# Both MLPs of a mixer from float16 parts, with the low-part matmuls one step behind

## The chip, the cores and the metric

The kernel runs on one core of a Trainium2 chip. The metric is device microseconds of one execution; the median of three executions stands for a kernel. The engines are named as in the profile: PE (TensorE, matmuls), PEld (its weight loads), DVE (VectorE), ACT (ScalarE), POOL (GpSimd) and SP (SyncE, which issues most DMAs). A program hands every engine its own list of instructions, which it works off in that order; semaphores make one engine wait for another.

## The reference

Four sequences of 768 positions and 384 features go through three layers. Only the two MLPs, which the change touches, are shown in full:

```python
# layer 1: linear attention with complex decay, y[t] = q[t] . S[t], S a 48x48 state per head
x = attention(q, k, v, a_re, a_im)            # (4, 768, 384)
# layer 2
u = x + (x^T @ U @ V)^T                        # U (768, 32), V (32, 768)
x = u + np.maximum(u @ w_ch1, 0.0) @ w_ch2     # w_ch1 (384, 1536), w_ch2 (1536, 384)
# layer 3, with its own w_ch1, w_ch2
u = x + real(fft(fft(x, axis=1), axis=2))
un = (u - mean(u)) / sqrt(var(u) + 1e-06)
out = u + np.maximum(un @ w_ch1, 0.0) @ w_ch2
```

The MLP weights, U and V come as float64, the rest as float32.

## The kernel before

**How an exact product is made.** An operand that needs more than one matmul pass of precision is split into a high part and the rest (hi + lo), both of type fp32r here, and a product is three matmuls: hi·hi, hi·lo, lo·hi. That is `mm3` (L91 to L95; the three matmuls are L93, L94, L95).

**The MLPs.** `moe_units` (L161) runs one MLP. The hidden width of 1536 is cut into 12 blocks `f` of 128, a sequence (`b`) into two halves `g` of 384 positions. For each (b, g, f), called a unit here: nine matmuls make the hidden block `hp` in PSUM (three blocks `k` of the input times `mm3`); ACT writes its positive part `hh` to SBUF (L191), DVE the remainder `hl` (L193); then `second` (L166) multiplies `hh` and `hl` with the block's second weight into three accumulators `acc` with nine more matmuls. `second` of a unit is issued after the nine `hp` matmuls of the next unit. A unit is 18 matmuls of 128 by 128 by 384; a pass (one b, one g) is 12 units, 216 matmuls; there are 16 passes, 3456 matmuls. `hp` has two PSUM banks, `hh` and `hl` two buffers each, `acc` three banks.

**What runs beside them.** The attention of the first sequence stands ahead of everything. During the first MLP's passes of sequence b the attention of sequence b+1 is worked in (`Side` counts out its steps, one or two a half unit), during the last sequence's passes the Fourier part `dft(0)`; during the second MLP's passes the Fourier part of the next sequence. `make_ut` and `make_un` build the input pairs `u` (hi, lo) of the next pass in its last units.

**The weights.** `load_w` (L138) brings half a block's weights: a DMA of float64 words `stw` (384 KB, into a ring of 5 buffers that the `u` pairs share), one ACT and three DVE operations that make a float32 `x` of them (L110, L132, L133; `x` is one of 3 buffers), an ACT copy that rounds the high part into `w` (L147) and a POOL subtraction for the low part (L148). There are 48 such loads, 24 for each MLP. A block's `w` tile (fp32r, high and low, both products) is one of 12 buffers, so all blocks of one MLP fill them: the second MLP's loads have to wait for the last pass of the first, where two a unit are asked for, and four come behind it.

**The order.** A list scheduler lays the instructions of each engine out in the order in which its own clock finds them ready, with `high_priority` for `hh` and `hl`. So work written later can come earlier on an engine that it finds free.

**At the end** `verdict` (L1012) counts range tests, each in a column of `stats`; only if one fails does a slow exact path (`recurrence`, `rest`) run.

## Time and profile before

| what | us |
|---|---|
| median of three executions (lowest, highest) | 1004.03 (1003.54, 1008.71) |
| the profiled execution, and its span in the trace | 1008.71, 1008.7 |
| attention of sequence 0, up to the first hp matmul | 0 to 139.6 |
| first MLP, sequences 0 to 2, with attention 1 to 3 | 139.6 to 553.4 |
| first MLP, sequence 3, and first pass of the second MLP | 553.4 to 708.3 |
| second MLP, its other seven passes, and the end | 708.3 to 1008.7 |
| PE, DVE, ACT, POOL busy over the span | 867.8, 643.1, 466.6, 224.9 |

The profiled execution is the slowest of the three, 4.7 us over the median. Busy time of PE counts matmuls that overlap as one stretch, so its share says where PE stood still, not how fast it went; that is read from the distance between starts of matmuls.

### The profile page before, as it was taken

To read this page: it belongs to the slowest core of one execution; us is meant where nothing else is said; L and a number is where in the kernel's file an instruction comes from. 1 tells how busy PE (TensorE), PEld (TensorE's weight loads), DVE (VectorE), ACT (ScalarE), POOL (GpSimd) and SP (SyncE) were. 2 spreads that over 40 slices of the span, in tenths; PEclk is the share of its full clock that TensorE was granted. 3 is DMA by queue.
4 is the path that set the end of the run, shared out by engine and by line. 5 is a ranking of instruction groups with operands and counts; after the bars stand their busy time and mean duration, and the time that the engine had idled before them with its cause. 6 is when DMAs were issued, how large, how long until landed. Compare 5 with 4: busy or idle time off the path is not lost.

```text
span 1008.7 us, 16225 instructions
## 1 busy us (share of the span) xinstructions
PE 867.8 (86%) x6350; PEld 821.9 (81%) x6350; DVE 643.1 (64%) x1110; ACT 466.6 (46%) x891; POOL 224.9 (22%) x227
## 2 busy tenths in 40 slices
PE   0056858798898898989999999799999999999997
PEld 0045747787887898878999999689999999999997
DVE  7967696767567796787873539986535635453121
ACT  8556557565775877768742223453112212211111
POOL 4312362302012010120205216532401312010000
PEclk9998677988998999989999999999999999999999
DMA  9049546463653627346055114341210101000000
GB/s 355 1 64 155 146 136 131 102 102 104 103 95 79 104 79 119 81 91 105 9 88 204 40 32 134 109 149 33 65 46 17 58 23 47 1 25 24 1 24 27
DMA packets 47093, 83.39 MB, mean 83 GB/s; under 512 B 5600, under 2 KB 36064, under 8 KB 47008
## 3 DMA queue, kind: packets, MB, share of 16 engines
q1 hardware_dynamic: 45152, 75.96, 33.3%
q0 software_dynamic: 1856, 6.31, 1.9%
q8 instruction: 52, 0.85, 0.4%
q14 instruction: 33, 0.27, 0.1%
HBM read 53.79 MB, written 9.44 MB: 63 GB/s over the span
## 4 chain that ended last, share of the span: by engine, by line
PE 46%; DVE 24%; DMA 13%; ACT 8%; issue 4%; SPq 4%; POOL 1%; another core or an unknown queue 0%; ACTq 0%; DVEq 0%; POOLq 0%
DMA QT<-QK 8%; PE acc L95 6%; PE hp L93 6%; PE hp L95 6%; PE hp L94 6%; PE acc L93 6%; PE acc L94 6%; DMA stw<-in_w_dram 5%; SPq L437 4%; PE sc L462 3%; DVE ls L354 2%; DVE QK L430 2%; DVE wxw L133 1%; ACT ls L89 1%; DVE wxw L132 1%
## 5 line engine op out<-in xcount | busy, mean ns | idle before, releaser
L193 DVE SCALAR_TENSOR_TENSOR hl<-hp,hh 128x384 fp32r<-128x384 f32 x192 | 105.6, 552 | 201.0 <-ACT hh L191 193.3
L191 ACT ACTIVATE hh<-hp 128x384 fp32r<-128x384 f32 x192 | 93.4, 488 | 273.9 <-PE hp L95 253.7
L93 PE MATMUL acc<-w,hh 128*128 128x384 f32 x576 | 204.0, 354 | 5.9 <-ACT hh L191 4.8
L94 PE MATMUL acc<-w,hh 128*128 128x384 f32 x576 | 198.8, 345 | 0.0
L95 PE MATMUL acc<-w,hl 128*128 128x384 f32 x576 | 164.7, 351 | 17.6 <-DVE hl L193 17.4
L95 PEld LDWEIGHTS acc<-w,hl 128*128 128x128 f32 x576 | 106.4, 194 | 23.6 <-DVE hl L193 23.1
L93 PEld LDWEIGHTS acc<-w,hh 128*128 128x128 f32 x576 | 111.8, 194 | 10.5 <-ACT hh L191 8.6
L94 PEld LDWEIGHTS acc<-w,hh 128*128 128x128 f32 x576 | 112.3, 195 | 0.2
L93 PE MATMUL hp<-u,w 128*128 128x384 f32 x288 | 101.2, 355 | 11.4 <-ACT u L639 11.4
L94 PE MATMUL hp<-u,w 128*128 128x384 f32 x288 | 103.2, 358 | 0.0
L95 PE MATMUL hp<-u,w 128*128 128x384 f32 x288 | 101.8, 353 | 0.0
L94 PE MATMUL hp<-n,w 128*128 128x384 f32 x288 | 96.5, 335 | 1.4 <-DVE n L917 1.2
L95 PE MATMUL hp<-n,w 128*128 128x384 f32 x288 | 96.5, 335 | 0.0
L93 PE MATMUL hp<-n,w 128*128 128x384 f32 x288 | 96.3, 335 | 0.0
L462 PE MATMUL sc<-QT 96*128 96x128 f32 x384 | 59.8, 311 | 28.7 <-DMA QT<-QK 23.5
L462 PEld LDWEIGHTS sc<-QT 96*128 96x128 f32 x384 | 55.1, 219 | 32.9 <-issue 30.3
L148 POOL TENSOR_TENSOR w<-wxw,w 128x384 fp32r<-128x384 f32 x48 | 57.5, 1202 | 75.1 <-ACT w L147 72.9
L93 PEld LDWEIGHTS hp<-u,w 128*128 128x128 f32 x288 | 57.7, 202 | 12.8 <-ACT u L639 12.8
L94 PEld LDWEIGHTS hp<-u,w 128*128 128x128 f32 x288 | 57.5, 200 | 1.1 <-DVE u L640 0.8
L95 PEld LDWEIGHTS hp<-u,w 128*128 128x128 f32 x288 | 57.3, 199 | 0.4
L94 PEld LDWEIGHTS hp<-n,w 128*128 128x128 f32 x288 | 54.1, 188 | 2.0 <-DVE n L917 2.0
L537 POOL TENSOR_SCALAR fe<-QT 96x8 f32<-96x8 f32 x20 | 6.5, 325 | 216.4 <-DMA QT<-QK 211.4
(285 smaller groups left out, 1747.3 us busy)
## 6 DMA issues: line engine op xcount, KB each, us to landing
QT<-QK SPq DMA_DIRECT2D x144, 129.0 KB
stw<-in_w_dram SPq DMA_DIRECT2D x48, 384.0 KB
ain<-in_a_dram SPq DMA_DIRECT2D x12, 768.0 KB
qkin<-in_qk_dram SPq DMA_DIRECT2D x12, 768.0 KB
x1d<-x SPq DMA_DIRECT2D x24, 192.0 KB
vin<-in_v_dram SPq DMA_DIRECT2D x18, 192.0 KB
lo<-x1d SPq DMA_DIRECT2D x12, 192.0 KB
out_dram<-lo SPq DMA_DIRECT2D x12, 192.0 KB
```

The lines of the kernel that those rows point to most:

```text
L89: ordered(lambda: A.activation(*args, **kw))
L93: T.matmul(o, ah, bh, start=start, stop=False, skip_group_check=skip)
L94: T.matmul(o, ah, bl, start=False, stop=False, skip_group_check=skip)
L95: T.matmul(o, al, bh, start=False, stop=stop, skip_group_check=skip)
L132: V.scalar_tensor_tensor(out=xi, in0=xi, scalar=3, in1=low, op0=ALU.logical_shift_left, op1=ALU.bitwise_or)
L148: G.tensor_tensor(w[:, 1, zs], x, f32(w[:, 0, zs]), ALU.subtract)
L191: A.activation(hh, hp, AF.Relu)
L193: V.scalar_tensor_tensor(out=hl, in0=hp, scalar=0.0, in1=f32(hh), op0=ALU.max, op1=ALU.subtract)
L354: V.tensor_tensor_scan(out=flat(s1), data0=starts, data1=flat(s1), initial=1.0, op0=ALU.max, op1=ALU.mult)
L430: V.tensor_tensor(QK[:, :, :, to], x[:, :, j].unsqueeze(1).to_broadcast([128, 2, 3, 128]), w, ALU.mult)
L437: nc.sync.dma_start(QT[p0 : p0 + 16], QK[:, z, i, :])
L462: T.matmul(ps[:, h, :], q[:, 128:256], q[:, :128], start=True, stop=True)
```

## The change

Both MLPs work on float16 parts instead of fp32r. Weights are scaled up before they are split (by 2^3 and 2^8, `WP`), the first MLP's input by 2^5 (`UP`), and the additions at the end scale back. For that each `load_w` has one more POOL operation, which scales `x` in place. The parts take half the room, so one buffer of `wpl` holds both MLPs' weights of a block (`wboth`), and the second MLP's loads are spread one a unit over sequence 3. New range tests: `check_v`, a square sum in `prelim`, and `check_w`, 48 DVE operations that square and sum the high parts. In `moe_units` the matmuls of `hl` go through a list `lows` and are issued one unit behind those of `hh`; `hl` has three buffers. The slow path keeps fp32r.

```diff
+    def hidden(name, tag):
+        if parts16[0]:
+            return moe.tile([128, 384], F16, tag=tag, name=name, bufs=3 if tag == "hl" else 2)
...
     def pair(name):
-        return moe.tile([128, 2, 384], F32R, tag="u", name=name, bufs=5)
+        return moe.tile([128, 2, 384], F16 if parts16[0] else F32R, tag="u", name=name, bufs=5)
...
     def load_w(mi, f, z, st=None):
-        if z == 0:
+        if z == 0 and not parts16[0]:
             wt[mi, f] = wpl.tile([128, 2, 768], F32R, tag="w", name=f"w{mi}_{f}")
+        elif z == 0:
+            if mi == 0:
+                wboth[f] = wpl.tile([128, 2, 2, 768], F16, tag="w", name=f"w{f}")
+            wt[mi, f] = wboth[f][:, mi]
...
-        A.copy(w[:, 0, zs], x)
-        G.tensor_tensor(w[:, 1, zs], x, f32(w[:, 0, zs]), ALU.subtract)
+        if parts16[0]:
+            A.activation(w[:, 0, zs], x, AF.Copy, scale=WP[z])
+            G.tensor_scalar(x, x, WP[z], 0.0, ALU.mult, ALU.add)
+            G.tensor_tensor(w[:, 1, zs], x, w[:, 0, zs], ALU.subtract)
...
+    def check_w(mi, f, z):
+
+        hi = wt[mi, f][:, 0, z * 384 : (z + 1) * 384]
+        unread = ft(f"chk{mi}_{f}_{z}", [128, 384], BF16, tag="chk", bufs=2)
+        at = stats[:, list(BOUNDS).index(("w1", "w2")[z]), mi * FB + f : mi * FB + f + 1]
+        V.scalar_tensor_tensor(out=unread, in0=hi, scalar=1.0, in1=hi, op0=ALU.mult, op1=ALU.mult, accum_out=at)
...
+        lows = []
+
+        def low(b, g, f, hl):
+            w2h = wt[mi, f][:, 0, 384:]
+            for t in range(3):
+                T.matmul(acc[t], hl[:, t * 128 : (t + 1) * 128], w2h, start=False, stop=f == FB - 1 and extra is None)
...
-            for t in range(3):
-                ts = slice(t * 128, (t + 1) * 128)
-                mm3(acc[t], (hh[:, ts], hl[:, ts]), (w2h, w2l), f == 0, f == FB - 1 and extra is None)
...
+            tss = [slice(t * 128, (t + 1) * 128) for t in range(3)]
+            for t, ts in enumerate(tss):
+                T.matmul(acc[t], hh[:, ts], w2h, start=f == 0, stop=False)
+                T.matmul(acc[t], hh[:, ts], w2l, start=False, stop=False)
+            lows.append((b, g, f, hl))
+            while len(lows) > (f < FB - 1 and parts16[0]):
+                low(*lows.pop(0))
...
-                        hh = moe.tile([128, 384], F32R, tag="hh", name=f"hh{mi}_{b}_{g}_{f}")
+                        hh, hl = (hidden(f"{x}{mi}_{b}_{g}_{f}", x) for x in ("hh", "hl"))
...
+        if parts16[0]:
+            A.activation(zp, zp, AF.Square, accum_out=stat("z", b, 0))
...
+                A.activation(zst[b], f32(zst[b]), AF.Copy, scale=UP * WP[0] * WP[1])
...
-        if not more and g == 1 and f >= 2:
-            load_w(1, f - 2, half)
-    for f in range(FB - 2, FB):
-        for z in range(2):
-            load_w(1, f, z)
+        if not more and half == 1:
+            load_w(1, g * 6 + f // 2, f % 2)
...
+        if b in (1, 2) and half == 1:
+            check_w(b - 1, f, g)
```

The first place is PE in the second MLP, sequence 1, second half, about block 7. Rows are the instructions in their order; a name's last number is a buffer. First as it was, the second product of block 7 whole and then block 9's hidden part:

```order
L93 MATMUL acc_1_1_2_8202<-w_7_6549,hh_1_1_7_8337 128x384
L94 MATMUL acc_1_1_2_8202<-w_7_6549,hh_1_1_7_8337 128x384
L95 MATMUL acc_1_1_0_8200<-w_7_6549,hl_1_1_7_8339 128x384
L95 MATMUL acc_1_1_1_8201<-w_7_6549,hl_1_1_7_8339 128x384
L95 MATMUL acc_1_1_2_8202<-w_7_6549,hl_1_1_7_8339 128x384
L93 MATMUL hp_1_1_9_8386<-n_1_0_7934,w_9_6654 128x384
L94 MATMUL hp_1_1_9_8386<-n_1_0_7934,w_9_6654 128x384
```

The same place in the changed kernel:

```order
L214 LDWEIGHTS hh_1_1_7_8416
L214 MATMUL acc_1_1_2_8274<-w_1173,hh_1_1_7_8416 128x384
L215 LDWEIGHTS hh_1_1_7_8416
L215 MATMUL acc_1_1_2_8274<-w_1173,hh_1_1_7_8416 128x384
L200 LDWEIGHTS hl_1_1_6_8392
L200 MATMUL acc_1_1_0_8272<-w_1045,hl_1_1_6_8392 128x384
L200 LDWEIGHTS hl_1_1_6_8392
L200 MATMUL acc_1_1_1_8273<-w_1045,hl_1_1_6_8392 128x384
L200 LDWEIGHTS hl_1_1_6_8392
L200 MATMUL acc_1_1_2_8274<-w_1045,hl_1_1_6_8392 128x384
L105 LDWEIGHTS w_1290
L105 MATMUL hp_1_1_9_8469<-n_1_0_7991,w_1290 128x384
```

Behind `hh` of block 7 now stand the low parts of block 6, and every matmul has a weight load of its own in the list, which with fp32r is part of the matmul.

The second place is DVE in the first MLP, sequence 2, second half, from block 6 on. Before:

```order
L193 SCALAR_TENSOR_TENSOR hl_2_1_6_5446<-hp_2_1_6_5382,hh_2_1_6_5444 128x384
L467 TENSOR_TENSOR pm_5_1_5369<-sc_5_1_5352,mask 128x512
L471 TENSOR_TENSOR ph_5_5351<-pm_5_1_5369,ph_5_5351 128x512
L193 SCALAR_TENSOR_TENSOR hl_2_1_7_5474<-hp_2_1_7_5459,hh_2_1_7_5472 128x384
L193 SCALAR_TENSOR_TENSOR hl_2_1_8_5499<-hp_2_1_8_5485,hh_2_1_8_5497 128x384
```

And after (`chk` is `check_w`'s output, `w` a block's weights):

```order
L233 SCALAR_TENSOR_TENSOR hl_2_1_6_5473<-hp_2_1_6_5410,hh_2_1_6_5472 128x384
L178 SCALAR_TENSOR_TENSOR chk_0_0_7665,stats<-w_598 128x384
L178 SCALAR_TENSOR_TENSOR chk_1_0_7721,stats<-w_715 128x384
L178 SCALAR_TENSOR_TENSOR chk_2_0_7752,stats<-w_831 128x384
L178 SCALAR_TENSOR_TENSOR chk_3_0_7795,stats<-w_931 128x384
L178 SCALAR_TENSOR_TENSOR chk_4_0_7824,stats<-w_990 128x384
L178 SCALAR_TENSOR_TENSOR chk_5_0_7857,stats<-w_1012 128x384
L178 SCALAR_TENSOR_TENSOR chk_6_0_7901,stats<-w_1045 128x384
L233 SCALAR_TENSOR_TENSOR hl_2_1_7_5501<-hp_2_1_7_5487,hh_2_1_7_5500 128x384
```

All 24 checks of the first MLP's weights, written into the second MLP's loop, come here, between block 6 and block 10; the 24 of the second MLP's weights come between sequence 3's first units and the second MLP's block 2.

The third place is POOL in the first MLP's loads, blocks 4 and 5. Before:

```order
L148 TENSOR_TENSOR w_4_982<-wxw_4_0_983,w_4_982 128x384
L148 TENSOR_TENSOR w_4_982<-wxw_4_1_992,w_4_982 128x384
L148 TENSOR_TENSOR w_5_1002<-wxw_5_0_1003,w_5_1002 128x384
L148 TENSOR_TENSOR w_5_1002<-wxw_5_1_1012,w_5_1002 128x384
L148 TENSOR_TENSOR w_6_1032<-wxw_6_0_1033,w_6_1032 128x384
```

After:

```order
L167 TENSOR_SCALAR wxw_4_0_991<-wxw_4_0_991 128x384
L168 TENSOR_TENSOR w_990<-wxw_4_0_991,w_990 128x384
L167 TENSOR_SCALAR wxw_4_1_1001<-wxw_4_1_1001 128x384
L168 TENSOR_TENSOR w_990<-wxw_4_1_1001,w_990 128x384
L167 TENSOR_SCALAR wxw_5_0_1013<-wxw_5_0_1013 128x384
```

Each load now has two POOL operations, and its `wxw` buffer is given back after the second.

## Rows read from the trace of the kernel before

**Rows 1.** The page: busy time by engine, and the granted clock by slices.

```profile
PE 867.8 (86%) x6350; PEld 821.9 (81%) x6350; DVE 643.1 (64%) x1110; ACT 466.6 (46%) x891; POOL 224.9 (22%) x227
...
PEclk9998677988998999989999999999999999999999
```

**Rows 2.** Stretches: length, busy PE, PEld, DVE, ACT, POOL, clock, DMA share, GB/s.

```profile
139.60:553.40 413.80, 370.04 (x3029) 344.12 (x3029) 300.64 (x449) 272.94 (x503) 76.10 (x64) 0.92 0.49 100
...
553.40:602.50 49.10, 47.62 (x298) 46.16 (x298) 22.78 (x48) 11.59 (x23) 7.26 (x10) 1.00 0.12 37
602.50:655.20 52.70, 46.28 (x254) 43.02 (x253) 50.29 (x107) 20.14 (x42) 32.56 (x34) 0.97 0.39 113
...
553.40:708.30 154.90, 145.35 (x856) 137.72 (x856) 112.67 (x226) 53.29 (x111) 56.13 (x62) 0.98 0.27 81
708.30:1008.70 300.40, 293.52 (x1771) 290.17 (x1769) 122.55 (x280) 58.95 (x124) 43.71 (x59) 0.99 0.09 30
```

**Rows 3.** Timeline of PE: start, length (us), operation; one unit, then two slow matmuls.

```profile
803.97 0.33 PE L93 MATMUL acc<-w,hh 128*128 128x384 f32 x1
...
807.09 0.33 PE L93 MATMUL hp<-n,w 128*128 128x384 f32 x1
...
637.23 0.53 PE L94 MATMUL hp<-u,w 128*128 128x384 f32 x1
637.55 0.53 PE L95 MATMUL hp<-u,w 128*128 128x384 f32 x1
```

**Rows 4.** Float16 matmuls: a run in PE's timeline, and the tile's durations (min/median/max ns).

```profile
125.10 4.09 PE L971 MATMUL warm<-ident,mask 128*128 128x256 f16 x36
...
L971 PE MATMUL warm<-ident,mask x76: 269/273/283, 70.6 to 134.5; 128*128 128x256 f16 x76
```

**Rows 5.** Who waited for whom (us, times, longest): 139 to 310, 310 to 555, 553 to 656.

```profile
PE hp L93 <- ACT u L639: 11.4, 3, 4.8
PE acc L95 <- DVE hl L193: 7.9, 3, 3.4
...
PE acc L95 <- DVE hl L193: 3.2, 3, 2.1
...
PE acc L95 <- DVE hl L193: 6.0, 5, 2.7
```

**Rows 6.** POOL by line (ns min/median/max, or busy us, mean ns); who L110 awaited.

```profile
L148 POOL TENSOR_TENSOR w<-wxw,w x48: 990/1024/2640, 105.1 to 691.0; 128x384 fp32r<-128x384 f32 x48
...
L537 POOL TENSOR_SCALAR fe<-QT 96x8 f32<-96x8 f32 x20 | 6.5, 325 | 216.4 <-DMA QT<-QK 211.4
...
  POOL w L148: 10.9, 8
```

**Rows 7.** DVE's part of a load: min/median/max ns; groups' means; one case in time.

```profile
L110 DVE TENSOR_SCALAR stw<-stw x48: 339/355/3489, 92.5 to 687.2; 128x384 int32<-128x384 int32 x48
L132 DVE SCALAR_TENSOR_TENSOR wxw<-wxw,stw x48: 537/548/1385, 97.1 to 689.2; 128x384 int32<-128x384 int32 x48
L133 DVE SCALAR_TENSOR_TENSOR wxw<-stw,wxw x48: 530/548/2154, 98.1 to 689.8; 128x384 int32<-128x384 int32 x48
...
L133 DVE SCALAR_TENSOR_TENSOR wxw<-stw,wxw 128x384 int32<-128x384 int32 x48 | 33.4, 701 | 0.4
L132 DVE SCALAR_TENSOR_TENSOR wxw<-wxw,stw 128x384 int32<-128x384 int32 x48 | 31.8, 663 | 2.9 <-ACT wxw L110 2.6
L110 DVE TENSOR_SCALAR stw<-stw 128x384 int32<-128x384 int32 x48 | 27.3, 568 | 16.8 <-DMA stw<-in_w_dram 16.7
...
182.58 3.49 DVE L110 TENSOR_SCALAR stw<-stw 128x384 int32<-128x384 int32 x1 [4.14 <-DMA stw<-in_w_dram]
183.09 1.81 POOL L352 TENSOR_TENSOR turn<-ain,turn 128x768 f32<-128x768 f32 x1
```

**Rows 8.** DVE groups of one shape by output type (busy us, mean ns, idle).

```profile
L193 DVE SCALAR_TENSOR_TENSOR hl<-hp,hh 128x384 fp32r<-128x384 f32 x192 | 105.6, 552 | 201.0 <-ACT hh L191 193.3
L482 DVE SCALAR_TENSOR_TENSOR k<-kp,k 128x384 f16<-128x384 f32 x40 | 21.3, 547 | 5.4 <-ACT k L481 5.3
```

55 lines of the change are left out of this document (43 added, 12 removed).

## The prediction

> **What bounds the kernel now.** I read the stretches first: they show where PE is full and where it stands still [rows 2]. From 708 us on PE is busy 293.5 of 300.4 us while DVE needs 122.6 and ACT 59.0: there the time is the number of matmuls times the distance between their starts. One unit of 18 matmuls takes 807.09 - 803.97 = 3.12 us, 0.173 us a matmul [rows 3]. From 139.6 to 553.4 PE is busy 370 of 413.8 us, DVE 301 and ACT 273: PE leads, but the attention of the next sequence makes it wait, and the granted clock is 0.92. At the low level a matmul takes 0.32 us, twice as long [rows 3], so the clock stands for 2 x 0.08 x 413.8 = 66 us at that level; the page shows the low slices in the first half of the span, where PE is least busy [rows 1]. From 553 to 708 us, where the second MLP's weights come in, DVE becomes full: 50.3 of 52.7 us from 602.5 on, and 112.7 of 154.9 in the whole stretch, PE 145.4. The waits say the same: PE stood waiting for `hl` 7.9, 3.2 and 6.0 us in the three parts [rows 5].
>
> **Cadence.** The matmuls that fill PE in float16 in the trace are those of 256 columns, 36 of which took 4.09 us from the first start to the last end; less the last one's 0.27, 35 distances are 3.82 us, 0.109 us each [rows 4]. Each of them has its own weight load in the list, as the changed kernel's have. For 384 columns that gives 0.164 us if all of it grows with the columns; half of the 0.32 us of a slow matmul is 0.160, the least if the streaming alone counts; and 0.173 if the type changes nothing. I take 0.163, 0.010 us less a matmul, because those runs are nearest in kind. At the low clock I count no gain.
>
> Behind 708 us there are 7 passes, 7 x 216 = 1512 matmuls: -15.1 us. At the very end the three additions now wait for three matmuls that stand together instead of three apart, so two of them no longer hide: three rows like [rows 8] begin some 0.3 us later each, +0.6. Sum **-14.5**. Nothing else is near there: float16 outputs cost DVE the same (547 against 552 ns [rows 8]).
>
> **The first MLP, sequences 0 to 2** (139.6 to 553.4). 1296 matmuls, of which 66 of 413.8 us, 16%, lie at the low clock: 1090 x 0.010 = 10.9 us if PE alone set the time. It is busy 89% and waits for ACT and DVE in between, whose work does not shrink: I count two thirds, **-7.3** (between 0 and -10.9).
>
> The late `hl`: before, the third matmul of a second product needed it. Now its first need is the release of its `hp` bank for the unit after next, which comes behind nine matmuls (six `hh`, three of the block before): seven matmuls later, 7 x 0.163 = 1.1 us more room. The six waits of 7.9 + 3.2 us can give back 6.6 us at most; a DVE that is behind stays behind, and `hh` keeps its old place, so **-4** (0 to -6.6).
>
> **The added POOL operation.** 48 scalings of 128 x 384 float32. The trace has none; the nearest rows are the two-input subtraction of the same size, 1.02 us, and a one-input scaling of 96 x 8, 0.33 us [rows 6]. I take 1.0, by the size. The Trainium skill (GPSIMD Engine Reference, Engine selection) holds one-input operations to run at about line rate and two-input ones to be some 2 times slower; by it the operation would be nearer 0.5 us (an estimate), and the sum 3 us lower; no run here shows it.
>
> POOL itself has room. What it does to DVE shows in the three DVE operations of a load: medians 355, 548, 548 ns, means 568, 663, 701, so 0.48 us a load are lost to waits in the operation, beside 1.2 us of POOL. One case shows it whole: L110 began at 182.58, lasted 3.49 us instead of 0.36, with POOL at work [rows 7]. Per us of POOL that is 0.4 us of DVE; 24 loads in the first MLP make 24 x 1.0 x 0.4 = 9.6 us. There the loads stand in one line with ACT, which also waited 10.9 us for a POOL subtraction to free an `x` buffer [rows 6], and PE 11.4 us for a `u` behind that ACT queue [rows 5]. I put half on the path, **+5** (0 to +24, all of POOL's time). The Trainium skill (SBUF — State Buffer, Who interferes with whom) speaks against the change at this place: a DVE instruction with two SBUF inputs, or in a 2-port mode, and a GpSimd one that reads SBUF exclude each other for a whole instruction. By that rule the loss goes with the number of meetings and not with 0.4; all 48 in full would be the slower rival below. The 3.49 us agree with it, the medians say that most miss each other.
>
> **The checks.** The 24 of the first MLP stand on DVE between blocks 6 and 10 of sequence 2's second half: 24 x 0.55 (the price of [rows 8]) = 13.2 us, with four `hl`, 2.2, and two other operations 16.5 us, against four units of 18 x 0.163 = 2.93 us, 11.7. The difference is 4.8, and attention matmuls and the longer room of `hl` cover part: **+2** (0 to +5). The 24 others fall into the next stretch. The square sums and the scaling of `zst` on ACT are eight operations of half a us in queues before `u` and the last-half additions: **+1** (0 to +2).
>
> **553 to 708 us.** 648 matmuls less 0.010 are -6.5, so PE alone would need 138.9 instead of 154.9: -16 at best. DVE would have 112.7 + 24 x 0.55 for the checks + 9.6 for POOL's other 24 scalings = 135.5: not more than PE on the whole. Before, the loads crowded into the half that was full; now half of those in sequence 3's two passes stand in the first one, where DVE had its room (112.7 less 50.3 is what the other two thirds of the stretch hold). The ring of 5 for `stw`, which `u` shares, keeps a load from coming when it is due, and DVE close to full keeps `hl` late at places. Between -16 and 0; **-10**.
>
> Sum: -14.5 - 7.3 - 4 + 5 + 2 + 1 - 10 = -27.8. In the profiled execution that is 1008.7 to 981. The median of the three is 1004.03; the same difference gives **976 us**.
>
> **Rivals.** (1) PE sets the time nearly everywhere: -14.5 - 10.9 - 6.6 - 16 + 1 = -47, 957 us. For it speaks PE's 89% and 94% in the two stretches; against it, that the waits name DVE and ACT, which get more to do. Chance 0.14. (2) The additions eat what the first MLP and the load stretch would give; the second MLP's -14.5 stays, with a few us either way: 985 to 1000, chance 0.09. (3) Float16 matmuls keep the distance of 0.173, because the pair of weight load and matmul sets it: -14.5, -7.3 and 6.5 of the -10 fall away, 1004. Against it: pairs at 0.109 us [rows 4]. Chance 0.05. (4) **Slower**: POOL's scaling lies fully on the path of each load, the subtraction and the DVE operations waiting behind it: 48 x 1.0 = 48 in place of the 5 and of what is in the -10, and the gains that are left are 14.5 + 6.5 + 7.3 + 4 = 32.3; with 3 for checks and squares +19, 1023 us. It decides from 0.6 us a load on. For it: the 10.9 and 3.49 us; against it: loads come some 4 us apart and have three `x` buffers. Chance 0.06. That a range test trips and the slow path runs I hold under 0.01: 384 squares of weights drawn with variance 1/384 add up to about 1 against a bound of 1.5; it would multiply the time.
>
> **How the numbers follow.** The forecast has 0.66, with 960 to 988 as its own range. The range of 8 in 10 has to take in rival 1 and most of 2: 950 to 994. A measurement of this kernel tells 0.5%, 5 us, from no change. Faster: 0.66 + 0.14 + 0.07 of rival 2 = 0.87. Within 0.5%: 0.02 of rival 2 + 0.05 = 0.07. Slower: 0.06.
>
> **What would show it.** In the profile after: a unit of the second MLP of 2.93 us, and the seven passes 15 us shorter; right or wrong, this is the first step to look at. PE's wait for `hl` at the low-part matmul gone, and a smaller one at the third next `hp`. POOL's new line near 1.0 us and L110, L132, L133 with larger means. The first MLP's sequences 0 to 2 5 us or less shorter as a sum; the stretch around sequence 3 near 145. If sequence 0's passes grow by more than 10 us, POOL is on the path and rival 4 has begun; if the first MLP shrinks by 15 us or more, I have taken DVE and ACT for more binding than they are.

## The result, and the profile after

The changed kernel takes **995.09 us** (median of four, 992.8 to 996.05) against 1004.38 us of the kernel before in the same comparison: 0.989 of its time, 95% interval 0.987 to 0.992. It is faster by 9.3 us. The forecast of 976 us had the sign right and the size three times too large; the time lies 1 us above the range of 950 to 994. It lies inside the second rival, 985 to 1000 us, which had a chance of 0.09.

The profiled execution of the changed kernel took 995.69 us; its span in the trace is 993.9 us, 14.8 less than the span of the kernel before (1008.7). The page first: busy time by engine, and the granted clock by slices. PEld, the weight loads, falls from 81% to 55% of the span, since a float16 load takes 0.10 us where an fp32r one took 0.19 to 0.20; PE itself falls from 867.8 to 819.1 us [rows 1].

```profile
PE 819.1 (82%) x6350; PEld 550.5 (55%) x6350; DVE 669.9 (67%) x1214; ACT 465.4 (47%) x897; POOL 259.9 (26%) x275
...
PEclk9999878888998999999989999999999999999999
```

The stretches, cut at the same places of the program as in [rows 2] (columns: stretch, length, busy PE, PEld, DVE, ACT, POOL, clock, DMA share, GB/s). The first is the first MLP's sequences 0 to 2, then the two passes of sequence 3, then both and the second MLP's first pass, then the other seven passes:

```profile
136.80:557.40 420.60, 351.35 (x3026) 240.60 (x3026) 314.65 (x498) 273.25 (x507) 89.99 (x80) 0.92 0.49 100
557.40:611.20 53.80, 47.38 (x298) 30.36 (x298) 43.28 (x92) 21.21 (x44) 24.96 (x28) 0.94 0.33 98
611.20:661.60 50.40, 41.75 (x254) 25.00 (x253) 48.51 (x111) 17.97 (x40) 41.68 (x45) 1.00 0.39 114
557.40:708.90 151.50, 134.84 (x855) 86.40 (x855) 122.41 (x279) 52.63 (x112) 74.53 (x85) 0.98 0.27 80
708.90:993.90 285.00, 276.70 (x1774) 176.56 (x1771) 124.14 (x284) 58.38 (x124) 43.92 (x60) 0.99 0.10 32
```

| stretch | before, us | after, us | difference | forecast |
|---|---|---|---|---|
| up to the first hp matmul | 139.6 | 136.8 | -2.8 | none |
| first MLP, sequences 0 to 2 | 413.8 | 420.6 | +6.8 | -3.3 |
| sequence 3 and the second MLP's first pass | 154.9 | 151.5 | -3.4 | -10 |
| the second MLP's other seven passes, the end | 300.4 | 285.0 | -15.4 | -14.5 |

All that is left at the end is what the second MLP gives. Up to 708 us the two kernels are level (708.3 and 708.9), although PE's busy time in the first MLP fell by 18.7 us (370.0 to 351.4).

The cadence is as forecast. PE in the second MLP, sequence 1 (start, length in us, operation), one unit from its first matmul to the next unit's:

```profile
802.55 0.33 PE L105 MATMUL hp<-n,w 128*128 128x384 f16 x1
...
805.48 0.33 PE L105 MATMUL hp<-n,w 128*128 128x384 f16 x1
```

805.48 - 802.55 = 2.93 us for 18 matmuls, 0.163 us each, against 0.173 in [rows 3].

Who made PE wait in the first MLP's sequences 0 to 2 (us, times, longest). Before, 137 to 557 us:

```profile
PE hp L93 <- ACT u L639: 11.4, 3, 4.8
PE acc L95 <- DVE hl L193: 11.1, 6, 3.4
PE acc L93 <- ACT hh L191: 4.3, 5, 2.2
```

After, the same stretch:

```profile
PE acc L214 <- ACT hh L232: 16.5, 7, 6.4
PE hp L105 <- ACT u L691: 8.3, 3, 3.5
```

The 11.1 us of waiting for `hl` are gone, as the later low parts were to do, and PE now waits 16.5 us for `hh` where it waited 4.3. The two sums, 15.4 and 16.5, are about the same: the wait got another name. That a unit's hidden block became ready no earlier is the likely reason; it was not traced.

POOL's new line (L167, the scaling), its old one (L168) and the first of DVE's three operations of a load (ns min/median/max):

```profile
L167 POOL TENSOR_SCALAR wxw<-wxw x48: 505/518/1530, 106.1 to 671.5; 128x384 f32<-128x384 f32 x48
L168 POOL TENSOR_TENSOR w<-wxw,w x48: 909/1090/2385, 107.2 to 672.4; 128x384 f16<-128x384 f32 x48
...
L122 DVE TENSOR_SCALAR stw<-stw x48: 312/362/2011, 92.4 to 667.9; 128x384 int32<-128x384 int32 x48
```

The scaling takes 0.52 us, not the 1.0 us that I took from the two-input row of [rows 6].

### The profile page after: what moved, and what is told of

It reads as the page before. It is cut to its first block, busy times and chain, and to the rows that moved or that the text cites. A ratio compares the mean times of both kernels' runs of the same rounds, so it can differ in the third digit from the quotient of the medians.

```text
span 993.9 us, 16380 instructions
## 1 busy us (share of the span) xinstructions
PE 819.1 (82%) x6350; PEld 550.5 (55%) x6350; DVE 669.9 (67%) x1214; ACT 465.4 (47%) x897; POOL 259.9 (26%) x275
## 4 chain that ended last, share of the span: by engine, by line
PE 37%; DVE 30%; DMA 13%; ACT 9%; issue 5%; SPq 3%; POOL 2%; DVEq 0%; ACTq 0%; POOLq 0%
DMA QT<-QK 8%; PE acc L214 5%; PE acc L200 5%; PE acc L215 5%; PE hp L105 5%; PE hp L107 5%; PE hp L106 5%; DMA stw<-in_w_dram 4%; SPq L481 3%; DVE ls L398 2%; DVE wxw L145 2%; DVE wxw L144 2%; PE sc L506 2%; DVE hl L233 2%; DVE chk L178 2%
## 5 line engine op out<-in xcount | busy, mean ns | idle before, releaser
L214 PE MATMUL acc<-w,hh 128*128 128x384 f16 x576 | 194.5, 338 | 26.4 <-ACT hh L232 25.1
L233 DVE SCALAR_TENSOR_TENSOR hl<-hp,hh 128x384 f16<-128x384 f32 x192 | 105.1, 550 | 156.1 <-ACT hh L232 155.3
L232 ACT ACTIVATE hh<-hp 128x384 f16<-128x384 f32 x192 | 92.7, 484 | 231.9 <-PE hp L107 214.2
L215 PE MATMUL acc<-w,hh 128*128 128x384 f16 x576 | 193.6, 337 | 0.0
L200 PE MATMUL acc<-w,hl 128*128 128x384 f16 x576 | 128.8, 332 | 1.0 <-DVE hl L233 1.0
L105 PE MATMUL hp<-u,w 128*128 128x384 f16 x288 | 95.1, 333 | 13.3 <-ACT u L691 8.3
L106 PE MATMUL hp<-u,w 128*128 128x384 f16 x288 | 95.4, 331 | 2.2 <-DVE u L692 2.2
L214 PEld LDWEIGHTS <-hh 128*128 128x128 f16 x576 | 57.9, 100 | 69.8 <-ACT hh L232 33.8
L105 PE MATMUL hp<-n,w 128*128 128x384 f16 x288 | 93.9, 326 | 1.5 <-DVE hl L233 1.5
L107 PE MATMUL hp<-u,w 128*128 128x384 f16 x288 | 94.7, 330 | 0.0
L106 PE MATMUL hp<-n,w 128*128 128x384 f16 x288 | 93.9, 326 | 0.0
L107 PE MATMUL hp<-n,w 128*128 128x384 f16 x288 | 93.9, 326 | 0.0
L106 PEld LDWEIGHTS <-w 128*128 128x128 f16 x576 | 56.7, 98 | 43.9 <-issue 10.2
L105 PEld LDWEIGHTS <-w 128*128 128x128 f16 x576 | 56.8, 99 | 43.3 <-issue 7.7
L200 PEld LDWEIGHTS <-hl 128*128 128x128 f16 x576 | 57.1, 100 | 41.6 <-issue 3.7
L107 PEld LDWEIGHTS <-w 128*128 128x128 f16 x576 | 56.7, 98 | 39.6 <-issue 4.3
L215 PEld LDWEIGHTS <-hh 128*128 128x128 f16 x576 | 58.0, 101 | 35.9 <-issue 6.4
L168 POOL TENSOR_TENSOR w<-wxw,w 128x384 f16<-128x384 f32 x48 | 54.1, 1131 | 3.1
```

The lines of the kernel that those rows point to most:

```text
L105: T.matmul(o, ah, bh, start=start, stop=False, skip_group_check=skip)
L106: T.matmul(o, ah, bl, start=False, stop=False, skip_group_check=skip)
L107: T.matmul(o, al, bh, start=False, stop=stop, skip_group_check=skip)
L168: G.tensor_tensor(w[:, 1, zs], x, w[:, 0, zs], ALU.subtract)
L200: T.matmul(acc[t], hl[:, t * 128 : (t + 1) * 128], w2h, start=False, stop=f == FB - 1 and extra is None)
L214: T.matmul(acc[t], hh[:, ts], w2h, start=f == 0, stop=False)
```

## The experiments

The first MLP shares its time with the attention of the next sequence. The question is which of the two sets it. **Theory A**: the attention does. It is one long line of steps: ACT and DVE make QK, SP issues six transfers that turn a chunk's QK into QT (a chunk is 128 positions; sequences 1 to 3 have 18), PE multiplies (`sc`), DVE masks, and so on to the next chunk. **Theory B** is the prediction's: PE sets it for two thirds. **Theory C**: PE sets it wholly. Beside these stand the rivals that name the additions: the range tests (D), the later low parts (E), the POOL scaling.

The medians are of 4 to 12 executions, beside executions of the kernel before, which took 1005.3, 1005.4, 1006.8, 1005.9 and 1005.9 us in the five comparisons.

### Less PE work in the first MLP

```diff
-                mm3(acc[t], (hh[:, ts], hl[:, ts]), (w2h, w2l), f == 0, f == FB - 1 and extra is None)
+                if mi == 0 and b != B - 1 and b != "r":
+                    T.matmul(acc[t], hh[:, ts], w2h, start=f == 0, stop=False)
+                    T.matmul(acc[t], hh[:, ts], w2l, start=False, stop=False)
+                else:
+                    mm3(acc[t], (hh[:, ts], hl[:, ts]), (w2h, w2l), f == 0, f == FB - 1 and extra is None)
```

> The kernel before, with less PE work in the first MLP: the matmuls of the low hidden part `hl` are left out in sequences 0 to 2 (36 a pass, 216 in all; this part of the product is missing from the output). `hl` is still made by DVE. 216 x 0.173 = 37.4 us less PE work at the fast rate, three and a half times what the float16 cadence takes off in this stretch. Theory A (the first MLP's sequences 0 to 2 are set by the attention of the next sequence, not by PE): at most a quarter of it shows, -10 us or less; 994 to 1004 us, and the stretch from the first hp to the end of sequence 2 stays above 404 us (413.8 before). Theory B (my prediction: two thirds of what PE saves shows): -25 us, about 979 us, the stretch near 389 us. Theory C (PE sets it): -37 us, 967 us.

Measured: 1007.0 us, ratio 1.001 (0.999 to 1.003). Nothing of 37 us shows. The stretch of the first MLP's sequences 0 to 2 in this run:

```profile
140.00:558.00 418.00, 356.57 (x2825) 326.54 (x2825) 294.40 (x447) 272.02 (x502) 66.50 (x55) 0.87 0.45 89
```

It is 418.0 us long, 413.8 before. Two things took the gain. PE's busy time fell by 13.5 us (370.0 to 356.6) and not by 37. The granted clock fell from 0.92 to 0.87: of the two levels, 1.2 and 2.4 GHz, the low one now holds 2 x 0.13 x 418 = 109 us in place of 66, and 43 us at 0.32 us a matmul in place of 0.173 [rows 3] cost about 20 of the 24 us that are missing (an estimate). And the 13.5 us that did fall became idle time. Two thirds of even 13.5 would be 9 us, and the stretch is 4 us longer: Theories B and C are out. Theory A's 994 to 1004 us was missed too, by 3 us on the slow side.

### The attention's transfers made twice

```diff
                         nc.sync.dma_start(QT[p0 : p0 + 16], QK[:, z, i, :])
+                        if b:
+                            nc.sync.dma_start(QT[p0 : p0 + 16], QK[:, z, i, :])
```

> The kernel before, with each of the six transfers of a chunk's QT made twice in sequences 1 to 3 (108 more issues on SP and 129 KB each; the result is the same). PE, DVE, ACT and POOL have the same work. Theory A (the attention chain sets the first MLP): 6 x 0.74 = 4.4 us more in a chunk, of 18 chunks half to all on the chain: +40 to +80 us, 1044 to 1084 us, all of it between 140 and 553 us of before. Theory B (PE at two thirds): the chain has slack, at most +25 us, 1005 to 1030 us. Theory C: 1005 us.

Measured: 1061.95 us, ratio 1.057 (1.052 to 1.061), +56.5 us. The first MLP's stretch is 464.9 us, 51.1 more, with the engines' work unchanged (PE's busy time grows by the clock, 0.87):

```profile
135.30:600.20 464.90, 387.34 (x3028) 361.95 (x3029) 296.71 (x455) 273.86 (x503) 75.59 (x66) 0.87 0.56 120
```

The chain of work that ended last, by line, as shares of that stretch; first the kernel before (139.6 to 553.4), then this run (the view ends its rows where they end here):

```profile
by line: DMA QT<-QK 12.2%; SPq L437 6.7%; issue 6.4%; DMA stw<-in_w_dram 3.8%; PE sc L462 3.7%; DVE ls L354 3.4%; ACT ls L89 3.4%; DVE QK L430 3.0%; DVE turn L396 3.0%; PE hp L93 2.4%; ACT turn L89 2.3%; PE hp L95 2.2%; PE acc L95 2.2%; PE 
```

```profile
by line: DMA QT<-QK 23.1%; PE y L492 3.9%; SPq L439 3.7%; issue 3.7%; PE sc L464 3.7%; DMA stw<-in_w_dram 3.4%; SPq L437 3.3%; DVE QK L430 3.1%; PE acc L95 2.6%; PE hp L93 2.4%; PE hp L94 2.4%; PE hp L95 2.4%; PE acc L93 2.2%; PE acc L94 2.
```

In the kernel before, the QT transfers and SP's issuing of them (L437) are 19% of the chain, and each line of the MLP's matmuls is 2.4% or less. This row was to be had before the prediction; the page's chain over the whole execution already named QT's transfers first, with 8%. Doubling the transfers adds 56.5 us: Theory A, within its range. The 108 added issues of 0.60 us, the median in the changed kernel, would be 65, but that agrees in size only: on the chain SP's issuing grew from 28 to 33 us (6.7% of 413.8, 3.7% and 3.3% of 464.9) and the transfers from 51 to 107 (12.2% and 23.1%). Nearly all of the added time is spent in the transfers themselves.

### The attention's transfers joined, two for six

```diff
+                if b:
+                    qt_, qk_ = QT.rearrange("p h t -> p (h t)"), QK.rearrange("p z i t -> p (z i t)")
+                    nc.sync.dma_start(qt_[:, :1548], qk_[:96])
+                    nc.sync.dma_start(qt_[:, 1548:], qk_[32:, :516])
```

(in sequences 1 to 3, in place of the six of a chunk)

> The kernel before with a chunk's QT of sequences 1 to 3 brought by two transfers in place of six, the same bytes in longer rows (the rows then stand in the wrong places of QT, so attention of these sequences is wrong; all engines have the same work). SP issues 4 fewer a chunk, 0.58 us each, 2.3 us sooner whole, and the transfers themselves may be shorter. Theory A (the attention chain sets the first MLP): 0.7 of 18 chunks on the chain, as the doubled transfers showed, gives -29 us from the issues alone: 960 to 980 us. If the chain is only just the bound, and PE or DVE stand right behind it: -3 to -12 us, 993 to 1002 us, as the pieces gave. Theories B and C: 1003 to 1007 us.

Measured: 983.61 us, ratio 0.978 (0.977 to 0.980), -22.3 us. With the same work on the engines, the first MLP's stretch falls by 23.3 us, the next one stays (153.7 against 154.9):

```profile
135.80:526.30 390.50, 356.43 (x3029) 334.29 (x3030) 300.64 (x451) 272.18 (x503) 83.07 (x66) 0.94 0.35 106
526.30:680.00 153.70, 143.51 (x856) 136.61 (x856) 111.01 (x224) 52.89 (x111) 53.85 (x60) 0.99 0.26 80
```

The chain of work that ended last in that stretch:

```profile
by line: issue 7.0%; DMA QT<-QK 6.7%; PE sc L466 4.6%; PE acc L95 4.2%; PE hp L93 4.0%; DMA stw<-in_w_dram 4.0%; PE hp L94 4.0%; PE hp L95 3.9%; PE acc L93 3.7%; PE acc L94 3.7%; DVE QK L430 3.4%; DVE turn L396 2.8%; PE y L494 2.4%; DVE ls 
```

SP's issuing no longer stands among the larger shares, the transfers have about half of theirs, and the six lines of the MLP's matmuls have grown from some 2% each to about 4%. By the chain PE comes next. The gain lies between the two that Theory A offered (29, and 3 to 12). Whether PE really is next, the same kernel with less PE work tells:

> Both edits in one: two transfers a chunk in place of six, and the first MLP's sequences 0 to 2 without the low hidden part's matmuls (216 fewer, 37.4 us of PE; that part of the product and the right places of QT are missing from the output). Tells whether PE stands right behind the chain. If the chain is still the bound after the first edit: the same as with the two transfers alone, within 3 us. If PE then sets the time: up to 37 us less than that.

Measured: 985.17 us, ratio 0.979 (0.978 to 0.981), no less than with the joined transfers alone. The stretch:

```profile
136.00:528.30 392.30, 340.20 (x2824) 313.14 (x2824) 301.54 (x446) 270.71 (x502) 71.48 (x57) 0.89 0.33 98
```

37.4 us of PE work less left 16.2 us less PE busy time, at a clock of 0.89 in place of 0.94, and no us of the stretch. So even with 23 us taken from the attention's line, the stretch does not wait for PE's matmuls. That it still waits for the attention is likely and not shown: no run shortens that line further. That PE lines make up a quarter of the chain says that the chain ran through PE's queue, not that shorter matmuls shorten it.

### Float16 in the second MLP alone

The edit goes from the kernel before: float16 `w`, `hh`, `hl` and `u` for the second MLP, its scaling and its scaled additions; nothing else.

```diff
+            if mi == 1 and parts16[0]:
+                wt[mi, f] = wpl_half(wt[mi, f])
...
-                        hh = moe.tile([128, 384], F32R, tag="hh", name=f"hh{mi}_{b}_{g}_{f}")
+                        kind = F16 if mi == 1 and parts16[0] else F32R
+                        hh = moe.tile([128, 384], kind, tag="hh", name=f"hh{mi}_{b}_{g}_{f}")
```

> The kernel before with float16 parts in the second MLP alone: the first MLP, its loads, the order of the second product, and the places of the loads stay as before; the second MLP's loads have the POOL scaling; the new range tests are left out. My prediction's terms for this part: -14.5 behind 708 us and 216 x 0.010 = -2.2 for the second MLP's first pass, +2 for 24 scalings: 990 us; the rest of the change was to bring 13 us more (27.8 forecast in all), so by it this kernel is 13 us slower than the changed one. Theory A (nothing that the change does up to 708 us shows): 986 to 993 us, the same as the changed kernel's 994.3 or a few us less, as the checks are not there.

Measured: 993.62 us, ratio 0.987 (0.984 to 0.990); the changed kernel, run again beside other experiments, had 994.25 and 0.989 (0.986 to 0.992). So what the change does up to 708 us is in sum worth nothing that can be measured. The stretches of this run (the same three as [rows 2] from the first):

```profile
135.60:552.80 417.20, 371.54 (x3029) 346.91 (x3029) 301.55 (x450) 273.11 (x503) 76.81 (x64) 0.91 0.49 99
552.80:709.90 157.10, 143.88 (x863) 123.69 (x863) 114.21 (x229) 53.33 (x112) 73.28 (x88) 0.97 0.27 80
709.90:994.40 284.50, 274.95 (x1764) 175.38 (x1762) 120.07 (x276) 58.42 (x123) 42.01 (x56) 1.00 0.10 32
```

Sequences 0 to 2 take 417.2 us with fp32r, 420.6 with float16. The next stretch takes 157.1 us, 151.5 in the changed kernel: there the change does bring something, and the checks take part of it, as shown below.

### The changed kernel again

Unedited, for the comparison:

> The changed kernel itself, for the comparison on one chip with the runs beside it: 993 to 997 us.

Measured: 994.25 us (993.43 to 997.34). Its first MLP took 415.3 us here and 420.6 in the first profile, with the same instructions. So 5 us of that stretch differ from one execution to the next, and the +6.8 of the table is not a loss that needs a cause of its own. The seven profiles with float16 in the first MLP and the attention as it was have 415.3 to 420.6 us there, the two with fp32r and all its matmuls 413.8 and 417.2: whatever float16 does in that stretch, it is no gain.

### Without the range tests on the weights, and with them held back

```diff
-        if b in (1, 2) and half == 1:
-            check_w(b - 1, f, g)
```

> The changed kernel without the 48 DVE operations of `check_w` (their range tests then count as kept). Theory A (attention sets the first MLP; the checks, 24 of which the order puts into sequence 2's second half, cost a little there): -3 to -6 us, 989 to 992 us, nearly all of it in that half pass (66.6 us long) and the stretch behind it. Theory D (the checks are where the missing gain of the load stretch went): -8 to -14 us, 981 to 987 us. Prediction's term: -2 in the half pass, and a few us up to 708 us.

```diff
         if b in (1, 2) and half == 1:
-            check_w(b - 1, f, g)
+            seen = [i for i in nc.cur_bb.bb.instructions if i.engine == V.engine][-1]
+            with tc.issue_after(seen):
+                check_w(b - 1, f, g)
```

> The changed kernel with all 48 `check_w` operations kept, each held behind the DVE instruction written just before it, so that they stay in the second MLP's loop, where DVE is busy 124 of 285 us. If DVE has room there and only the place of the checks costs: the same time as without them, within 2 us (989 to 992 by theory A, 981 to 987 by theory D). If a check costs by itself wherever it stands (48 x 0.56 = 27 us of DVE): 995 us as the changed kernel, or more.

Measured: 990.33 us without them (0.984, 0.981 to 0.988) and 990.89 with all 48 held in the second MLP (0.985, 0.982 to 0.988). The ratios' intervals overlap with the changed kernel's (0.986 to 0.992), but the stretch of sequence 3 and the second MLP's first pass tells them apart: it takes 151.5 to 153.7 us in the four profiles with the checks where the change puts them, and 143.4 to 149.3 in the six without them or with them held. So their place costs about 4 us, they themselves nothing: with the checks in it the second MLP takes 285.6 us, without them 286.0. The expectation named sequence 2's second half and the stretch behind it. It is not in the first: without the checks that half pass takes 66.1 us, with them 66.6. It is in the stretch behind. Without the checks:

```profile
556.70:702.50 145.80, 134.34 (x856) 86.88 (x855) 105.88 (x224) 52.47 (x112) 67.50 (x84) 0.98 0.28 84
```

With the checks held, that stretch and the second MLP's seven passes:

```profile
552.30:698.40 146.10, 134.42 (x857) 86.79 (x856) 106.83 (x224) 52.11 (x112) 67.89 (x84) 0.98 0.28 84
698.40:984.00 285.60, 276.79 (x1773) 176.54 (x1771) 145.94 (x380) 58.38 (x124) 44.77 (x60) 0.99 0.10 32
```

That is 145.8 and 146.1 in place of 151.5 us. By passes, first without the checks (sequence 3's two, the second MLP's first), then the last of these with them:

```profile
556.70:606.50 49.80, 46.28 (x298) 30.23 (x297) 36.75 (x76) 21.22 (x44) 22.29 (x28) 0.97 0.36 109
606.50:656.80 50.30, 42.70 (x254) 25.53 (x252) 46.58 (x99) 18.03 (x40) 39.27 (x46) 0.97 0.39 109
656.80:702.50 45.70, 45.36 (x308) 31.11 (x306) 22.55 (x52) 13.22 (x28) 5.94 (x11) 1.00 0.08 29
```

```profile
661.60:708.90 47.30, 45.70 (x306) 31.04 (x306) 30.62 (x78) 13.45 (x28) 7.89 (x13) 1.00 0.06 22
```

With the checks the first two passes take 53.8 and 50.4 us, as shown further up. So the checks cost 4.0 us in the first pass and 1.6 in the third, and nothing in the second, where DVE is fullest. Why the first, which has five checks of its own and comes behind the block of 24, loses most was not tried.

### The second product in its old order

```diff
-            for t, ts in enumerate(tss):
-                T.matmul(acc[t], hh[:, ts], w2h, start=f == 0, stop=False)
-                T.matmul(acc[t], hh[:, ts], w2l, start=False, stop=False)
-            lows.append((b, g, f, hl))
...
+            for t in range(3):
+                ts = slice(t * 128, (t + 1) * 128)
+                mm3(acc[t], (hh[:, ts], hl[:, ts]), (w2h, w2l), f == 0, f == FB - 1 and extra is None)
```

> The changed kernel with the second product in the order of the kernel before: hh, hh, hl for each of the three accumulators, all in one unit, no low part issued later. Everything else as changed. My prediction's step (the late low part gives back 4 us of the waits for hl in the first MLP, 0 to 6.6, and part of the load stretch): 999 to 1004 us. Theory A (those waits were in the shadow of the attention, the waits move from hl to hh and to the hp bank): within 3 us of the changed kernel, 992 to 998. Theory E (the late low part makes it worse): 985 to 991 us.

Measured: 991.43 us, ratio 0.986 (0.983 to 0.989), where the changed kernel has 0.989 (0.986 to 0.992): the intervals overlap, no difference is shown, and the 4 us that the prediction counted for the later low parts are not there. (991.43 lies just outside Theory E's 985 to 991 and below Theory A's 992 to 998; if anything, the old order is faster.) Its first MLP takes 416.3 us, 420.6 and 415.3 in the two profiles of the changed kernel, and PE waits there 13.8 us for `hh` and 8.6 for `hl`, in the first profile of the changed kernel 16.5 and 1.0. With the checks held as well:

> Both single edits that were faster than the changed kernel in one: the checks held in the second MLP, and the second product in the old order. If the two gains (3.4 and 2.8 us against 994.3) come from different places they add: 987 to 989 us. If both come from the same few us in sequence 2's second half and behind it: 990 to 992 us.

Measured: 990.68 us (0.983, 0.980 to 0.986), the same as with the checks held alone. The two do not add.

### Without the POOL scaling

```diff
-WP = 2.0**3, 2.0**8
+WP = 1.0, 1.0
...
-            G.tensor_scalar(x, x, WP[z], 0.0, ALU.mult, ALU.add)
```

> The changed kernel without the POOL scaling of each load (48 operations) and with the two weight scales at 1 (the low parts then lose digits in float16). My prediction's term, half of the DVE time that POOL takes away, was +5 us at 1.0 us an operation; at the 0.52 us that the profile after shows it is +2.5. Theory A (the loads of sequence 0 run beside the attention chain, which sets the time): 0 to -4 us, 991 to 995 us. Rival 4 of the prediction in small (POOL on the path of each load): 24 to 48 x 0.52 = -12 to -25 us, 970 to 983 us.

Measured: 994.72 us, ratio 0.989 (0.986 to 0.992), the same as with it. POOL's busy time in the first MLP's stretch falls from 91.6 to 76.7 us, and nothing follows.

### Half of the transfers from ACT's queue

```diff
-                        nc.sync.dma_start(QT[p0 : p0 + 16], QK[:, z, i, :])
+                        (nc.scalar if b and z else nc.sync).dma_start(QT[p0 : p0 + 16], QK[:, z, i, :])
```

> The changed kernel with the checks held in the second MLP, and with three of the six transfers that make a chunk's QT from QK issued by ACT's queue in place of SP's, for sequences 1 to 3 (SP takes 0.74 us an issue, 12 in 8.93 us). Theory A (the attention chain sets the first MLP): a chunk's QT is whole about 2.2 us earlier; the chain that ended last goes through some 9 to 18 such transfers in sequences 0 to 2, so -10 to -30 us against the 990.9 us without the split: 961 to 981 us. Theory B or C (PE sets it): no gain, 989 to 993 us. A rival: the three issues stand on ACT in front of hh, and PE waits for that: 54 x 0.74 = 40 us more on ACT, 990 to 1010 us.

Measured: 1019.68 us, ratio 1.013 (1.009 to 1.016), 29 us slower than with all on SP (990.89; the checks are held in both). The first MLP's stretch is 443.7 us long; in its part from 300 to 581 us PE waited 19.8 us for QT, 2.3 us in the kernel with the checks held from 300 to 557. The instructions of the attention also moved between the passes, since the scheduler that lays out the order saw other queues, so this run has two differences in it. It missed all three ranges, Theory A's 961 to 981 by most, and does not tell the theories apart; the rival on ACT was nearest to it in size.

### QK made in pieces

```diff
-                    V.tensor_tensor(QK[:, :, :, to], x[:, :, j].unsqueeze(1).to_broadcast([128, 2, 3, 128]), w, ALU.mult)
...
+                    for i in range(3):
+                        for to, x in ((slice(128, 256), kf), (slice(0, 128), qf)):
+                            V.tensor_tensor(QK[:, :, i, to], x[:, i, j].unsqueeze(1).to_broadcast([128, 2, 128]), w[:, :, i], ALU.mult)
+                        for z in range(2):
+                            p0 = z * 48 + i * 16
+                            nc.sync.dma_start(QT[p0 : p0 + 16], QK[:, z, i, :])
```

First in the changed kernel with the checks held:

> The changed kernel with the checks held, and QK of sequences 1 to 3 made by DVE in three pieces: each piece is two products of 256 columns instead of a third of two products of 768, and its two transfers are issued right behind it, so SP's six issues of 0.74 us begin after a third of the DVE work. The same bytes, the same number of transfers, 72 more DVE operations of some 0.35 us where 36 of 0.94 us were (hardly any DVE time more). Theory A (the attention chain sets the first MLP): 1 to 1.3 us less a chunk, at 0.7 of 18 chunks on the chain (as the doubled transfers showed: 56.5 of 79 us), -12 to -17 us against 990.9: 974 to 979 us. Theories B and C (PE sets it): 990 to 992 us. If the order of the engines changes with it, some us either way.

Measured: **981.15 us**, ratio 0.974 (0.971 to 0.978): the fastest of all, 9.7 us less than the 990.89 without the pieces. Where it comes from shows at one pair of chunks, DVE's products and SP's issues (start, length in us). In the changed kernel:

```profile
208.93 1.83 DVE L474 TENSOR_TENSOR QK<-ls,turn 128x768 f32<-128x768 f32 x2 [0.81 <-ACT turn L101]
...
210.78 8.79 SPq L481 DMA_DIRECT2D QT<-QK  x12
```

With the pieces:

```profile
211.44 3.77 DVE L479 TENSOR_TENSOR QK<-ls,turn 128x256 f32<-128x256 f32 x11
...
211.88 8.19 SPq L482 DMA_DIRECT2D QT<-QK  x12
```

There the issues begin 1.85 us after the products, here 1.24 us after the first of them, which stands alone at 210.64, and 0.44 after the rest. A piece takes 0.42 us and not the expected 0.35, and the 108 of them keep DVE busy for 38.1 us where the 36 did for 33.1; still the kernel gains. The gain is under the expected 12 to 17, and the profiles do not put it all into the first MLP: with the pieces it is 413.8 us there and 143.4 in the next stretch, against 415.5 and 146.1 without them. The edit also moved 14 of PE's instructions from the next stretch into the first (3040 in place of 3026). Differences of 5 us between executions allow no finer reading; so this run gives the fastest of the kernels that compute the whole, and for Theory A it is weak evidence beside the doubled and the joined transfers.

Then the same with the old order of the second product:

> The kernel of the run before this one with the second product in the old order too: by theory A the order of the low parts counts for little, within 3 us of it, 971 to 980 us.

Measured: 996.23 us, ratio 0.988 (0.985 to 0.991), 15 us slower, far outside the 3 us expected. Beside the same kernel without the pieces (990.68) it is 5.5 us slower: in the old order the pieces cost time. Its first MLP is 423.3 us against 413.8, its next stretch 148.4 against 143.4. The edit also lets the scheduler lay attention and MLP into each other in another way, and no run parts that from the low parts themselves. What the later low parts do is therefore settled only so far: nothing in two kernels, 15 us in a third.

### The pieces without the change, and with half of it

> The kernel before with nothing but the pieces of QK (made in three pieces, the transfers of each issued right behind it, sequences 1 to 3). Theory A (the attention chain set the first MLP before the change as well): about the -10 us that the pieces brought in the changed kernel with held checks: 993 to 998 us. If the chain became the bound only by the change (float16 took PE out of the way): 1003 to 1007 us.

The edit is the one above, made in the kernel before. Measured: 1001.21 us, ratio 0.996 (0.995 to 0.998). That lies between the two ranges. There is a gain, so the chain counted before the change as well, but it is 4.7 us and not 10; that the chain set the first MLP is shown by the doubled and the joined transfers, not by this run.

> Both edits in one: float16 parts in the second MLP alone, and the pieces of QK. If the two gains are apart in place they add: 976 to 983 us, as fast as the changed kernel with held checks and pieces (981). If with a shorter attention chain the first MLP's matmuls begin to set its time, this kernel, whose first MLP has fp32r matmuls, is slower than that by up to 11 us: 985 to 992 us.

Float16 in the second MLP alone, with the pieces. Measured: 988.2 us, ratio 0.983 (0.981 to 0.985): 5.4 us less than without the pieces, 7 more than the 981.15 with float16 in both. By the total the second expectation fits; by the stretches it does not. First the fastest kernel, from the first MLP's start on, then this one:

```profile
136.80:550.60 413.80, 351.65 (x3040) 237.89 (x3039) 305.36 (x524) 273.64 (x507) 83.82 (x77) 0.92 0.50 97
550.60:694.00 143.40, 131.56 (x843) 84.99 (x842) 109.63 (x228) 51.98 (x112) 73.55 (x89) 0.99 0.32 98
```

```profile
138.70:548.10 409.40, 363.48 (x3028) 337.24 (x3029) 308.63 (x528) 271.86 (x503) 83.74 (x68) 0.92 0.52 102
548.10:703.20 155.10, 143.22 (x859) 123.32 (x858) 109.22 (x219) 52.84 (x111) 66.92 (x83) 0.97 0.26 78
```

The first MLP's sequences 0 to 2 are no slower with fp32r (409.4) than with float16 (413.8). The difference is the next stretch, 155.1 against 143.4 us. There the change is worth 8 to 12 us (143.4 against 151.7 in the kernel before with the pieces and 155.1 here), about the 10 that the prediction said, once the checks are out of the way. Which of its parts does it (the cadence of sequence 3's 432 matmuls, 4.3 us by 0.010 each; the loads spread over both passes; the low parts) was not tried apart.

## Why the prediction was wrong

**The second MLP: right.** -14.5 forecast, -15.4 measured, by the mechanism named: 0.163 us a matmul, PE full, DVE at 124 of 285 us.

**The first MLP, sequences 0 to 2: the step that failed.** "It is busy 89% and waits for ACT and DVE in between, whose work does not shrink: I count two thirds, -7.3", and -4 for `hl`. PE's share says how little it stood still, not that the end of the stretch waits for it. The stretch ends when the attention of the next sequence is through, a line of dependent steps in which QT's transfers and their issues alone are 19%; I read the chain of waits for PE's waits and did not read the chain of work that ended last for this stretch. The runs show it four ways, all of them made from the kernel before: 37 us of PE work less, ratio 1.001; 108 transfers more, +56.5 us; two for six of them, -22.3 us, and 37 us of PE work less on top of that, nothing; the first MLP left at fp32r, 417.2 us for this stretch and 993.6 us in all, as with the whole change. In the changed kernel PE is busy 18.7 us less there, all of it turned into idle time. -11.3 became nothing.

The 4 us for `hl` failed in the same way and once more: PE's waits for `hl` went, and PE waited as long for `hh`. A wait is worth its length only if nothing else holds back what comes next.

**The POOL scaling: mis-sized, and without the loss it was to bring.** +5, from 1.0 us an operation and 0.4 us of DVE for each us of POOL, half of it on the path. 0.52 us was measured, and taking it out gave 0 (994.72 against 994.25). DVE's three operations of a load did not grow (busy us, mean ns, idle):

```profile
L145 DVE SCALAR_TENSOR_TENSOR wxw<-stw,wxw 128x384 int32<-128x384 int32 x48 | 34.3, 717 | 0.4
L144 DVE SCALAR_TENSOR_TENSOR wxw<-wxw,stw 128x384 int32<-128x384 int32 x48 | 34.2, 713 | 1.0 <-ACT wxw L122 0.7
L122 DVE TENSOR_SCALAR stw<-stw 128x384 int32<-128x384 int32 x48 | 24.1, 502 | 19.5 <-DMA stw<-in_w_dram 19.4
```

Their means add up to 1.93 us, as before [rows 7]. The Trainium skill (GPSIMD Engine Reference, Engine selection) holds one-input operations on GpSimd to be roughly at line rate; the 0.52 us, about half of the two-input 1.09, agree with it. The row that I went by, a two-input one, was the wrong neighbour.

**The checks: the wrong place.** +2 in sequence 2's second half, where they cost nothing that shows, and nothing of their own charged behind it. They cost 5.7 us in the next stretch. The step was that DVE's 135.5 us there are "not more than PE on the whole": a sum over 155 us. DVE measured less, 122.4 us, and the checks cost time all the same, 4.0 us in the first of the three passes, where DVE is busy 43.3 of 53.8 us. The second, with 48.5 of 50.4 us, lost nothing: neither the sum nor the share of a pass says where a wait falls.

**553 to 708 us:** -10 forecast, -3.4 measured, -9 with the checks away (154.9 to 145.8 or 146.1). The size was right for what the stretch would give without them. The +1 for the square sums and the scaling of `zst` was not tried apart.

**From profile to median.** The two spans differ by 14.8 us, the medians by 9.3. The kernel before was profiled in its slowest execution, 4.3 us over the median of 1004.38, the changed one 0.6 over its own; and 993.9 is a span, 1.8 under the time of its execution, while for the kernel before both are 1008.7. I carried the whole difference over to the median: 5.5 us more than the runs bear out.

Together: 27.8 forecast; 10.1 missing in the first MLP, 6.6 in the next stretch, 0.9 more in the second MLP, 2.8 more before the first matmul give the 14.8, and 5.5 between profile and median the 9.3. Of the 10.1 the wrong mechanism is the smaller part: gains of 11.3 and costs of 8 were counted, neither came, and by luck that leaves 3.3. The other 6.8 is the +6.8 of the table, which was +1.5 in another execution (415.3 us). The 2.8 are no gain of the change either: the first `hp` matmul comes at 135.3 to 140.0 us in kernels of both sorts. The second rival named this outcome, and its cause holds in part: the checks ate 5.7 us of what the load stretch would give, but in sequences 0 to 2 there was no gain to eat.

## What to carry to other kernels

Where two strands of work share a stretch, read which of them its end waits for, from the chain of work that ended last over that very stretch, before a gain is counted from an engine's busy share: 89% busy was worth nothing here, while the strand that is 19% transfers and their issues gave -22 and +56 us. The chain points at a strand and does not price it: with the joined transfers PE's matmuls were a quarter of the chain, and 37 us less of them gave nothing. A cheap trial of that question is to lengthen one strand by a known amount. Work without a deadline, as range tests are, belongs where its engine has room in that very pass, and a scheduler that lays it wherever the engine is momentarily free has to be held back.

## What the runs showed of the hardware

**The clock can take back.** With 216 matmuls fewer in the first MLP, PE was granted less: 0.87 in place of 0.92, and 0.89 in place of 0.94 with the joined transfers. It was 0.87 too with the transfers doubled, where PE stood still for 78 us in place of 44. It is not so each time: in the changed kernel PE stood still for 69 us of that stretch and had 0.92, as before. In the second MLP, where it runs nearly without gaps, all kernels had 0.99 or 1.00. Work taken from an engine that waits for others can be partly paid back in slower matmuls.

**One check of 3.61 us.** DVE's checks take 0.55 us; one took 3.61, and 0.28 us behind its start POOL began three two-input operations in a row (start, length in us; DVE, then POOL):

```profile
551.81 3.61 DVE L178 SCALAR_TENSOR_TENSOR chk<-w 128x384 bf16<-128x384 f16 x1
```

```profile
552.09 1.00 POOL L881 TENSOR_TENSOR xe<-lo,hi 128x384 f32<-128x384 f32 x1
553.05 0.99 POOL L883 TENSOR_TENSOR xo<-lo,hi 128x384 f32<-128x384 f32 x1
554.01 0.98 POOL L885 TENSOR_TENSOR ye<-x,x 128x384 f32<-128x384 f32 x1
```

DVE's operation ends at 551.81 + 3.61 = 555.42, 0.43 us behind the third of POOL's (554.99). The same place in the second profile of the changed kernel:

```profile
550.04 1.34 DVE L178 SCALAR_TENSOR_TENSOR chk<-w 128x384 bf16<-128x384 f16 x1
551.32 1.34 DVE L178 SCALAR_TENSOR_TENSOR chk<-w 128x384 bf16<-128x384 f16 x1
552.59 1.34 DVE L178 SCALAR_TENSOR_TENSOR chk<-w 128x384 bf16<-128x384 f16 x1
```

```profile
549.85 1.12 POOL L881 TENSOR_TENSOR xe<-lo,hi 128x384 f32<-128x384 f32 x1
550.93 1.30 POOL L883 TENSOR_TENSOR xo<-lo,hi 128x384 f32<-128x384 f32 x1
552.20 1.31 POOL L885 TENSOR_TENSOR ye<-x,x 128x384 f32<-128x384 f32 x1
```

Here the two engines took turns: each check ends 0.41 to 0.43 us behind the POOL operation that had begun before it, and POOL's operations are longer than the 0.98 to 1.00 us above. The Trainium skill (SBUF — State Buffer, Who interferes with whom) says that a DVE instruction with two SBUF inputs and a GpSimd one that reads SBUF exclude each other for a whole instruction; both profiles agree, and add that the same instructions of the same kernel met as turns in one execution and as one wait behind three in the other. What decides between the two was not tried. The median of the 48 checks is 0.55 us; eight of them took 0.79 us or more in the first profile.
